# Transposing x by DMA instead of on TensorE, in a kernel that mixes a spectral filter and a dense layer

## The chip, the cores and the metric

The kernel runs on one core of a Trainium2 chip. Its engines are TensorE (PE; its weight loads are listed apart as PEld), VectorE (DVE), ScalarE (ACT), GpSimd (POOL) and SyncE (SP). SP, ACT and POOL also issue DMA transfers; each has a queue of its own, and all transfers run on the same 16 DMA engines. On-chip memory is SBUF; PE writes to PSUM, of which a bank holds 128 partitions x 512 numbers of 32 bits.

The metric is the time of one execution in microseconds (us). An execution under the profiler gives a span (first to last event) and the records quoted below.

## The reference

Input x has 2048 rows of 512 values (bf16). The output mixes two branches with a gate per row:

```python
g = sigmoid((x * gate_w).sum(-1, keepdims=True))
X = rfft2(x);  a = irfft2(X * (w_r + 1j*w_i))          # 2048 x 257 spectrum
h = x @ w1 + b1                                        # 512 -> 1792
b = (h * tanh(softplus(h))) @ w2                       # 1792 -> 512 (the activation is Mish)
out = g * a + (1 - g) * b
```

## The kernel before

x's 2048 rows are cut into 16 tiles of 128 rows (tile t holds the rows p*16 + t, p being the partition). The work falls into these steps; the names are those of the code.

- **Loads.** SP's queue brings x by rows into `xo` (`ld_x`, five transfers), w1 (`ld_w1`, four), the constants of the transforms (`ld_fd`, `ld_m1`, `ld_sm`, `ld_gd`) and the gate's weights. POOL's queue brings the filter W (`ld_W`, four transfers to 64 partitions each, 64 rows of 8224 bytes) and w2 (`ld_w2`, two). These wait for the last transfer of w1.
- **Transposes** (`tr`, L522). For each tile four 128x128 transposes on PE, by a matmul against a permutation matrix, into PSUM; DVE or ACT evicts them (`evx`) into `xT`, which has the 512 columns of x on partitions, as four blocks of 128.
- **First transform, over the columns.** For each pair of tiles DVE forms sums and differences of the four blocks (`ty`, `tz`, `t0`, `t2`), for each tile PE multiplies by cosines and sines (`a1`, L551 to L554) into bank 0, and an eviction (`e1`) writes `In1`.
- **s1** (L572): after every four tiles, a transform over 64 of the rows' index positions, evicted (`e2`) to `Ybuf` and written to a scratch tensor in DRAM (`r1w`, two transfers of 256 KB for each s1, eight in all, in pieces of 512 bytes).
- **s2** (L689): when all eight `r1w` have landed, the scratch is read back in another order (`r1r`, four transfers of 512 KB; the first s2 needs two of them), transformed over the remaining 32 positions, multiplied by W (`wm`, `wz` on DVE and POOL), transformed back (`s2i`, L732), and written to a second scratch (`r2w`). There are four rounds. A small piece, `s2x`, follows the first s2 and needs all of `r1r`.
- **s1i, a1i** (L764, L776): the second scratch is read back (`r2r`) and transformed back; ACT scales by the gate (`geo`) and DVE or POOL combine the halves (`ga`).
- **Dense branch.** `mm1` (L810): 56 outputs, each of four matmuls of 512 columns, to banks 6 and 7 in turn; `mish` on ACT writes `act`, with the bias b1 that a small PE transpose (`tr_small`, L529) turned into a column. `mm2` (L851, and L833 for the last tile, in halves): 14 matmuls for each tile.
- **Gate.** 16 dot products on DVE (`gdot`, from `xo`), a reorder by two tiny DMAs (`gdj`), a sigmoid (`gcol`) and `omg` = 1 - gate.
- **End.** For the first NBF = 12 tiles `mm2` is evicted scaled by `omg` (`bev`, into `xo`), and later summed with `ga` (`sum`); for the others one instruction does both (`fin`). The results are stored (`out`) by SP and, for the last tile, ACT.

The order of the instructions on each engine is fixed when the kernel is built, by a planner. Each step is a task with an estimated duration, priority and dependences that come from the tiles it reads and writes. `_Graph.schedule` repeatedly takes, among the tasks that can start within 0.1 us of the earliest, the one with the highest priority. Where a step may run on two engines, it goes to the one that would be done first. Transfers of a queue keep the order in which they were written; the planner models SP's and ACT's as one pipe and POOL's as a second, separate one, with a bandwidth given by each transfer (`bw`). Warm-up matmuls (L509) on a tile of zeros fill PE until the first `mm1`. At run time an engine works through its list in order and waits at semaphores; an instruction that waits holds all behind it on its engine.

Of the kernel before, what the change touches and what calls it, by code (L numbers as in the profile page):

```python
# [13 lines left out]
NT = 16  # L14
# [303 lines left out]
NBF = 12  # L318
# [4 lines left out]
def _build(nc, A_x, A_w_r, A_w_i, B_x, B_w1, B_b1, B_w2, gate_w, out):  # L323
# [11 lines left out]
    with es:  # L335
# [4 lines left out]
        xT = sb("xT", [128, 4, NT, 128], BF)  # L340
# [22 lines left out]
        pid = sb("pid", [128, 142], BF)  # L363
        perm, id14 = pid[:, 0:128], pid[0:14, 128:142]
# [35 lines left out]
        xv = A_x[0].rearrange("(p t) d -> p t d", t=16)  # L400
        ov = out[0].rearrange("(a b t) d -> b a t d", b=2, t=16)
# [15 lines left out]
        def dma(name, dst, src, reads=(), writes=(), nbytes=0, deps=(), is_out=False, prio=None, queue="sp", bw=300e3):  # L417
            dur = 1.0 if queue == "pool" else 0.5

            def fn(e, _dst=dst, _src=src):  # L420
                return e.dma_start(_dst, _src)

            t = G.add(name, queue, dur, fn, reads=reads, writes=writes, lat=2.0 + nbytes / bw, deps=deps, prio=prio)
            t.xfer = nbytes / bw
            t.isdma = True
            if is_out:
                t.sem = out_sem
                n_out_dma[0] += 1
                t.semval = 16 * n_out_dma[0]
            else:  # L430
                t.sem = new_sem("d_" + name)
                t.semval = 16
            return t

        def mm(n):
            return n / 2400.0 + 0.0025
# [13 lines left out]
        def evict(name, n, dst, src, reads, writes, prio=None):  # L450
# [6 lines left out]
        G.add("ones", "pool", 0.2, lambda e: e.memset(pid[:, :], 1.0), writes=["ones"])  # L457
        G.add("perm", "pool", 0.3, lambda e: e.affine_select(out=perm[:, :], in_=perm[:, :], pattern=[[-1, 2], [-2, 64]],
                                                             compare_op=ALU.is_equal, fill=0.0, base=0, channel_multiplier=1),
              reads=["ones"], writes=["perm"])  # L460
# [4 lines left out]
        def ld_x(t0, t1):  # L465
            dma(f"ld_x{t0}", xo[:, t0:t1, :], xv[:, t0:t1, :], writes=[("x", t) for t in range(t0, t1)], nbytes=128 * 1024 * (t1 - t0),
                bw=260e3 if t0 < 4 else 380e3)
# [12 lines left out]
        ld_x(0, 1)  # L480
        ld_x(1, 4)
# [4 lines left out]
        ld_x(4, 8)  # L486
        ld_m1(0)
        ld_w1(2)
        ld_x(8, 12)
        t_w1 = ld_w1(3)  # L490
        ld_x(12, 16)
# [8 lines left out]
        WALL = [("W", i, h) for i in range(2) for h in range(2)]  # L500
        for h in range(2):
            dma(f"ld_w2_{h}", w2_sb[:, 7 * h:7 * (h + 1), :], w2v[:, 7 * h:7 * (h + 1), :],
                writes=[("w2", h)], nbytes=128 * 7 * 1024, queue="pool", deps=[t_w1])
# [11 lines left out]
        t_r1w = []  # L515
        for t in range(NT):
            tbk = 1 + t if 1 <= t < 4 else 1

            def f_tr(e, t=t, tbk=tbk):
                ins = None  # L520
                for dt_ in range(4):
                    ins = e.transpose(psb[:, tbk, 128 * dt_:128 * (dt_ + 1)], xo[:, t, 128 * dt_:128 * (dt_ + 1)], perm[:, :])  # L522
                return ins

            t_tr = pe(f"tr{t}", 4 * mm(128), f_tr, reads=[("x", t), "perm"], writes=[("bank", tbk)], prio=SP0 + 1.0)
            evict(f"evx{t}", 512, xT[:, :, t, :], psb[:, tbk, 0:512].rearrange("p (r j) -> p r j", r=4),
                  [("bank", tbk)], [("xT", t)], prio=SP0 + 1.0)
            if t == 3:
                pe("tr_small", 0.1, lambda e: e.transpose(psb[:, 0, 0:14], braw[0:14, :], id14[:, :]),  # L529
                   reads=["braw", "id14"], writes=[("bank", 0)], deps=[t_tr], prio=SP0 + 1.0)  # L530
                G.add("ev_small", "dve", 0.2, lambda e: e.tensor_copy(out=b1f[:, :], in_=psb[:, 0, 0:14]), reads=[("bank", 0)], writes=["b1f"], prio=SP0 + 1.0)

            if t % 2 == 1:
# [6 lines left out]
                lo, hi = xT[:, 0:2, t0:t0 + 2, :], xT[:, 2:4, t0:t0 + 2, :]  # L540
                yy = yb[:, yi, :, :].rearrange("p r (t j) -> p r t j", t=2)
                xr = [("xT", t0), ("xT", t)]
# [5 lines left out]
        for t in range(NT):  # L548
            def f_a1(e, t=t):
                pr = ps[:, 0, :].rearrange("p (r x) -> p r x", r=4)  # L550
                e.matmul(pr[:, 0, :], Tb[:, 0, t, :], FDs[:, 0:128], start=True, stop=True)  # L551
                e.matmul(pr[:, 2, :], Tb[:, 1, t, :], FDs[:, 128:256], start=True, stop=True)
                for i in range(2):
# [5 lines left out]
               writes=[("bank", 0)], prio=SP0)  # L559
            evict(f"e1_{t}", 512, In1[:, t, :].rearrange("p (c r q) -> p c r q", c=2, r=4),  # L560
                  ps[:, 0, :].rearrange("p (r c q) -> p c r q", r=4, c=2),
                  [("bank", 0)], [("In1", t)], prio=SP0 + 0.2)
# [237 lines left out]
        for c in range(NCH):  # L800
            hb = c % 3
            G.cur_prio = PR['mm1c0'] if c == 0 else PR['mm1c'] - c
            for ft in range(NFT):
# [3 lines left out]
                def f_mm1(e, c=c, ft=ft, bank=bank):  # L807
                    ins = None
                    for dt_ in range(4):
                        ins = e.matmul(ps[:, bank, :], w1_sb[:, dt_, 128 * ft:128 * (ft + 1)],  # L810
                                       xT[:, dt_, 4 * c:4 * c + 4, :], start=(dt_ == 0), stop=(dt_ == 3))
                    return ins

                t_mm1 = pe(f"mm1_{c}_{ft}", 4 * mm(512), f_mm1,
                   reads=[("xT", 4 * c + i) for i in range(4)] + [("w1", ft)], writes=[("bank", bank)])
                if c == 0 and ft == 0:
                    G.filled = t_mm1
                G.add(f"mish_{c}_{ft}", "act", act_dur(512, True),
# [162 lines left out]
```

## Time and profile before

| | us |
|---|---|
| median of 3 runs (lowest, highest) | 142.38 (142.08, 142.75) |
| the profiled execution | 142.56 |
| its span | 140.8 |
| PE busy | 136.2 (97%) |
| DVE / ACT / POOL busy | 86.3 / 81.4 / 31.9 |
| bytes moved by DMA | 21.38 MB, 152 GB/s over the span |
| granted PE clock | 1.0 throughout |

The page lists the busy time of each engine and then the span in 40 slices of 3.52 us; a digit is the busy share in tenths. PE's times overlap, because matmuls are pipelined: one of 512 columns is listed with 380 ns, while in the chain four of them take 0.86 us. The chain that ended last follows the work back from the end, always to what released it. In the DMA view q1 is the hardware queue of SP, q0 the software queue of POOL, and a row of digits gives the busy share of the 16 engines in 40 equal parts of the stretch asked for. A DMA issue line gives the number of transfers, KB each, and the median time from issue to landing. A timeline line gives the start, the duration, the engine (SPq for SP's queue), the source line and what is written from what.

### The profile page before, as it was taken

The page shows a single profiled execution, that of the slowest core. Times are in us where ns is not written, and L with a number is a line of the kernel's source. Part 1 is how long each engine was busy: PE and PEld are TensorE (multiplying, and loading weights), DVE is VectorE, ACT ScalarE, POOL GpSimd, SP SyncE. Part 2 cuts the span into 40 slices and gives each one's busy share as a digit, 9 for nine tenths or more (in the row PEclk, how much of TensorE's full clock was granted, in tenths as well). Part 3 has the DMA queues.
Part 4 walks back from the last instruction along what each step waited for, and adds up shares of the span by engine and source line. Part 5 has one row for each costly group of instructions (what it writes and reads, how often), then busy time and mean ns, then how long its engine had stood idle before and what let it go on. Part 6 is the DMA issues. An engine that isn't in the chain of part 4 may idle for free.

```text
span 140.8 us, 2515 instructions
## 1 busy us (share of the span) xinstructions
PE 136.2 (97%) x946; PEld 74.2 (53%) x946; DVE 86.3 (61%) x192; ACT 81.4 (58%) x128; POOL 31.9 (23%) x62
## 2 busy tenths in 40 slices
PE   6999999999999999999999999999999999999991
PEld 4756656455544435435445444544444666766670
DVE  0276757748999303983983893592200499999831
ACT  4448797969874487488058437532411685776300
POOL 4000670003000001560440440340000144256400
PEclk9999999999999999999999999999999999999999
DMA  3999999999705485700300300300359615333422
GB/s 87 334 382 387 393 245 214 239 333 366 222 8 154 151 254 202 289 0 10 143 0 0 149 0 5 149 2 0 143 150 277 179 27 119 80 79 92 98 52 58
DMA packets 16556, 21.38 MB, mean 152 GB/s; under 512 B 1248, under 2 KB 12384, under 8 KB 16160
## 3 DMA queue, kind: packets, MB, share of 16 engines
q1 hardware_dynamic: 15552, 17.22, 39.3%
q0 software_dynamic: 832, 3.94, 10.4%
q8 instruction: 7, 0.11, 0.3%
q10 hardware_dynamic: 160, 0.07, 0.2%
q14 instruction: 5, 0.04, 0.1%
HBM read 14.92 MB, written 6.29 MB: 151 GB/s over the span
## 4 chain that ended last, share of the span: by engine, by line
PE 92%; ACT 4%; DVE 0%; issue 0%
PE ps L810 33%; PE ps L851 32%; PE ps L776 5%; PE ps L509 3%; PE ps L689 3%; PE ps L572 3%; PE ps L732 3%; PE ps L764 3%; PE ps L522 2%; ACT Ybuf L452 2%; PE ps L833 2%; PE ps L554 2%; ACT act L819 1%; PE ps L551 1%; ACT Abuf L452 1%; ACT xT L452 1%
## 5 line engine op out<-in xcount | busy, mean ns | idle before, releaser
L810 PE MATMUL ps<-xT,w_sb 128*128 128x512 bf16 x224 | 54.2, 380 | 0.4 <-ACT act L819 0.3
L819 ACT ACTIVATE act<-ps,b1f 128x512 bf16<-128x512 f32 x56 | 38.1, 690 | 21.8 <-PE ps L810 16.4
L851 PE MATMUL ps<-w_sb,act 128*128 128x512 bf16 x210 | 48.3, 379 | 0.0
L810 PEld LDWEIGHTS ps<-xT,w_sb 128*128 128x128 bf16 x224 | 20.0, 98 | 24.1 <-ACT act L819 5.7
L851 PEld LDWEIGHTS ps<-w_sb,act 128*128 128x128 bf16 x210 | 20.1, 98 | 22.4 <-issue 0.4
L699 DVE TENSOR_TENSOR misc<-ps,WT 128x512 f32<-128x512 f32 x32 | 19.9, 685 | 12.6 <-PE ps L689 12.6
L705 POOL TENSOR_TENSOR misc<-misc 128x255 bf16<-128x255 f32 x16 | 11.4, 731 | 41.0 <-DVE misc L699 41.0
L784 POOL TENSOR_TENSOR Tg<-misc 128x256 bf16<-128x256 f32 x12 | 10.3, 873 | 27.9 <-ACT misc L781 27.9
L790 ACT ACTIVATE xo<-ps,omg 128x512 bf16<-128x512 f32 x11 | 7.6, 687 | 15.2 <-PE ps L851 15.0
L451 DVE CAST Ybuf<-ps 128x512 bf16<-128x512 f32 (+1 forms) x10 | 8.8, 900 | 9.3 <-PE ps L732 8.2
L781 ACT ACTIVATE misc<-ps,gcol 128x512 f32<-128x512 f32 x16 | 10.3, 685 | 5.0 <-PE ps L776 4.0
L451 DVE CAST misc<-ps 128x512 bf16<-128x512 f32 x8 | 5.5, 683 | 11.4 <-PE ps L764 11.4
L784 DVE TENSOR_TENSOR Tg<-misc 128x256 bf16<-128x256 f32 x20 | 12.0, 629 | 0.7 <-ACT misc L781 0.7
L594 DVE SCALAR_TENSOR_TENSOR junk<-xo,gwb 128x512 bf16<-128x512 bf16 x16 | 11.0, 689 | 0.7
L452 ACT ACTIVATE Ybuf<-ps 128x512 bf16<-128x512 f32 (+1 forms) x14 | 9.4, 718 | 2.6 <-PE ps L572 1.6
L451 DVE COPY xT<-ps 128x512 bf16<-128x512 bf16 x10 | 4.2, 424 | 9.1 <-PE ps L522 9.0
L776 PE MATMUL ps<-GDs,misc 128*128 128x256 bf16 x64 | 9.3, 273 | 0.0
L452 ACT ACTIVATE Abuf<-ps 128x512 bf16<-128x512 f32 x12 | 7.2, 602 | 0.0
L776 PEld LDWEIGHTS ps<-GDs,misc 128*128 128x128 bf16 x64 | 6.0, 98 | 2.3
L522 PEld LDWEIGHTS ps<-pid,xo 128*128 128x128 bf16 x64 | 5.2, 110 | 3.0 <-issue 0.4
L522 PE MATMUL ps<-pid,xo 128*128 128x128 bf16 x64 | 6.7, 242 | 0.0
L705 DVE TENSOR_TENSOR misc<-misc 128x255 bf16<-128x255 f32 x16 | 6.4, 441 | 0.0
(81 smaller groups left out, 115.7 us busy)
## 6 DMA issues: line engine op xcount, KB each, us to landing
scr<-Ybuf SPq DMA_DIRECT2D x8, 256.0 KB, 9.3
Abuf<-scr SPq DMA_DIRECT2D x4, 512.0 KB, 4.5
scr<-Ybuf SPq DMA_DIRECT2D x4, 512.0 KB, 3.0
Abuf<-scr SPq DMA_DIRECT2D x8, 256.0 KB, 5.3
w_sb<-in_B_w_dram POOLq DMA_DIRECT2D x2, 896.0 KB, 17.5
out_dram<-xo SPq DMA_DIRECT2D x14, 128.0 KB, 2.3
w_sb<-in_B_w_dram SPq DMA_DIRECT2D x3, 512.0 KB, 7.9
xo<-in_A_x_dram SPq DMA_DIRECT2D x3, 512.0 KB, 8.7
```

The source lines that it names most:

```text
L451: G.add_multi(name, [("dve", dve_dur(n), lambda e: e.tensor_copy(out=dst, in_=src)), ("act", act_dur(n), lambda e: e.activation(dst, src, ...
L452: ("act", act_dur(n), lambda e: e.activation(dst, src, AF.Copy))],
L522: ins = e.transpose(psb[:, tbk, 128 * dt_:128 * (dt_ + 1)], xo[:, t, 128 * dt_:128 * (dt_ + 1)], perm[:, :])
L594: lambda e, t=t: e.scalar_tensor_tensor(out=junk[:, :], in0=xo[:, t, :], scalar=1.0, in1=gwb[:, :], op0=ALU.mult, op1=ALU.mult, accum_out= ...
L699: lambda e, Pb=Pb, Wu=Wu, bk=bk, pb=pb: e.tensor_tensor(out=Pb[:, pb, :].rearrange("p (c r q) -> p c r q", c=2, r=4), in0=ps[:, bk, :].rea ...
L705: fz = (lambda e, c=c, Pb=Pb, op=op, pb=pb, i=i, zb=zb: e.tensor_tensor(out=Zb[:, zb, i, c, 1:256], in0=Pb[:, pb, 1:256], in1=Pb[:, pb, 25 ...
L776: ins = e.matmul(ps[:, yk, 256 * (j // 2):256 * (j // 2) + 256], TT[:, ts_, j, :], GDs[:, j, :], start=(j % 2 == 0), stop=(j % 2 == 1))
L781: lambda e, t=t, gb=gb, yk=yk: e.activation(gEO[:, gb, :], ps[:, yk, :], AF.Copy, scale=gcol[:, t:t + 1]),
L784: fg = (lambda e, i=i, op=op, t=t, gb=gb: e.tensor_tensor(out=ga[:, t, 256 * i:256 * i + 256], in0=gEO[:, gb, 0:256], in1=gEO[:, gb, 256:5 ...
L810: ins = e.matmul(ps[:, bank, :], w1_sb[:, dt_, 128 * ft:128 * (ft + 1)], xT[:, dt_, 4 * c:4 * c + 4, :], start=(dt_ == 0), stop=(dt_ == 3))
L819: lambda e, ft=ft, bank=bank, hb=hb: e.activation(act[:, hb, ft, :], ps[:, bank, :], AF.Mish, bias=b1f[:, ft:ft + 1]),
L851: ins = e.matmul(ps[:, bank, :], act[:, hb, ft, 128 * tl:128 * (tl + 1)], w2_sb[:, ft, :], start=(ft == 0), stop=(ft == NFT - 1))
```

## The change

The 64 PE transposes of x, their permutation matrix and their 16 evictions are removed. Eight DMA transfers issued on ACT's queue, ahead of everything else there, read 64 rows x 2048 values (four tiles) of x each and write them transposed into `xT`, whose two middle dimensions change places so that a tile's four blocks lie together. The column sums on DVE and `mm1` read `xT` in the new layout.

`xo` is no longer loaded first. x is loaded by rows in four transfers of 512 KB on POOL's queue, after W and before w2, for the gate's dot products alone (and since `xo` holds results later). SP's queue has no transfer of x left, so w1 and the constants move up, and the third part of w1 now goes ahead of the first part of the constant M1.

`a1` writes banks 0 and 1 in turn. The bias transpose uses bank 5 and comes after the first `mm1`. NBF is 10. The planner is told 500 GB/s for x's and w2's transfers on POOL's queue and 250 GB/s for the transposing ones. The planner's new order follows from all of this: on PE 24 warm-ups, then `mm1` twice, four `a1`, and so on; all of s1 is placed earlier among the `mm1` than before, the first s2 comes after 27 `mm1` groups (of four matmuls) and no `mm2`, where before 33 groups of `mm1` and three of the half tiles of `mm2` (seven matmuls each) stood ahead of it. The last `mm2` tiles stand together at the end. On SP, `gdj` comes behind the first `r2w` instead of between the `r1r`.

```diff
@@ -315,7 +315,7 @@
-NBF = 12
+NBF = 10
 NWARM = 40
@@ -337,7 +337,7 @@
         xo = sb("xo", [128, NT, 512], BF)
-        xT = sb("xT", [128, 4, NT, 128], BF)
+        xT = sb("xT", [128, NT, 4, 128], BF)
         Tg = sb("Tg", [128, 8192], BF)
@@ -360,8 +360,7 @@
         omg = sb("omg", [128, NT], F32)
-        pid = sb("pid", [128, 142], BF)
-        perm, id14 = pid[:, 0:128], pid[0:14, 128:142]
+        id14 = sb("id14", [14, 14], BF)
         wrv = sb("wrv", [128, 2, 2, 16], BF)
@@ -398,6 +397,7 @@
         xv = A_x[0].rearrange("(p t) d -> p t d", t=16)
+        xtv = A_x[0].rearrange("(a b t) d -> b a (t d)", b=2, t=16)
         ov = out[0].rearrange("(a b t) d -> b a t d", b=2, t=16)
@@ -414,11 +414,11 @@
-        def dma(name, dst, src, reads=(), writes=(), nbytes=0, deps=(), is_out=False, prio=None, queue="sp", bw=300e3):
+        def dma(name, dst, src, reads=(), writes=(), nbytes=0, deps=(), is_out=False, prio=None, queue="sp", bw=300e3, transpose=False):
             dur = 1.0 if queue == "pool" else 0.5
             def fn(e, _dst=dst, _src=src):
-                return e.dma_start(_dst, _src)
+                return e.dma_start_transpose(_dst, _src) if transpose else e.dma_start(_dst, _src)
@@ -454,17 +454,16 @@
         G.cur_prio = 99.0
-        G.add("ones", "pool", 0.2, lambda e: e.memset(pid[:, :], 1.0), writes=["ones"])
-        G.add("perm", "pool", 0.3, lambda e: e.affine_select(out=perm[:, :], in_=perm[:, :], pattern=[[-1, 2], [-2, 64]],
-                                                             compare_op=ALU.is_equal, fill=0.0, base=0, channel_multiplier=1),
-              reads=["ones"], writes=["perm"])
+        G.add("ones", "pool", 0.2, lambda e: e.memset(id14[:, :], 1.0), writes=["ones"])
         G.add("id14", "pool", 0.2, lambda e: e.affine_select(out=id14[:, :], in_=id14[:, :], pattern=[[1, 14]],
-        def ld_x(t0, t1):
-            dma(f"ld_x{t0}", xo[:, t0:t1, :], xv[:, t0:t1, :], writes=[("x", t) for t in range(t0, t1)], nbytes=128 * 1024 * (t1 - t0),
-                bw=260e3 if t0 < 4 else 380e3)
+        def ld_xt(g):
+            for bx in range(2):
+                dma(f"ld_xt{g}{bx}", xT[:, 4 * g:4 * g + 4, :, 64 * bx:64 * bx + 64].rearrange("p t r j -> p (t r) j"),
+                    xtv[bx, :, 2048 * g:2048 * g + 2048], writes=[("xT", t, bx) for t in range(4 * g, 4 * g + 4)], nbytes=128 * 2048,
+                    queue="act", bw=250e3, transpose=True)
@@ -477,18 +476,17 @@
-        ld_x(0, 1)
-        ld_x(1, 4)
+        ld_xt(0)
         dma("ld_b1", braw[:, :], B_b1.rearrange("(ft p) -> ft p", p=128), writes=["braw"], nbytes=3584, queue="pool")
         ld_w1(1)
-        ld_x(4, 8)
+        ld_xt(1)
+        ld_w1(2)
+        ld_xt(2)
         ld_m1(0)
-        ld_w1(2)
-        ld_x(8, 12)
+        ld_xt(3)
         t_w1 = ld_w1(3)
-        ld_x(12, 16)
         ld_m1(1)
@@ -498,9 +496,13 @@
         WALL = [("W", i, h) for i in range(2) for h in range(2)]
+        for t0 in range(0, NT, 4):
+            dma(f"ld_x{t0}", xo[:, t0:t0 + 4, :], xv[:, t0:t0 + 4, :], writes=[("x", t) for t in range(t0, t0 + 4)], nbytes=128 * 4096,
+                queue="pool", deps=[t_w1], bw=500e3)
         for h in range(2):
             dma(f"ld_w2_{h}", w2_sb[:, 7 * h:7 * (h + 1), :], w2v[:, 7 * h:7 * (h + 1), :],
-                writes=[("w2", h)], nbytes=128 * 7 * 1024, queue="pool", deps=[t_w1])
+                writes=[("w2", h)], nbytes=128 * 7 * 1024, queue="pool", deps=[t_w1], bw=500e3)
@@ -513,23 +515,10 @@
         t_r1w = []
+        t_small = pe("tr_small", 0.1, lambda e: e.transpose(psb[:, 5, 0:14], braw[0:14, :], id14[:, :]),
+                     reads=["braw", "id14"], writes=[("bank", 5)], prio=SP0 + 2.0)
+        G.add("ev_small", "dve", 0.2, lambda e: e.tensor_copy(out=b1f[:, :], in_=psb[:, 5, 0:14]), reads=[("bank", 5)], writes=["b1f"], prio=SP0 + 2.0)
         for t in range(NT):
-            tbk = 1 + t if 1 <= t < 4 else 1
-            def f_tr(e, t=t, tbk=tbk):
-                ins = None
-                for dt_ in range(4):
-                    ins = e.transpose(psb[:, tbk, 128 * dt_:128 * (dt_ + 1)], xo[:, t, 128 * dt_:128 * (dt_ + 1)], perm[:, :])
-                return ins
-            t_tr = pe(f"tr{t}", 4 * mm(128), f_tr, reads=[("x", t), "perm"], writes=[("bank", tbk)], prio=SP0 + 1.0)
-            evict(f"evx{t}", 512, xT[:, :, t, :], psb[:, tbk, 0:512].rearrange("p (r j) -> p r j", r=4),
-                  [("bank", tbk)], [("xT", t)], prio=SP0 + 1.0)
-            if t == 3:
-                pe("tr_small", 0.1, lambda e: e.transpose(psb[:, 0, 0:14], braw[0:14, :], id14[:, :]),
-                   reads=["braw", "id14"], writes=[("bank", 0)], deps=[t_tr], prio=SP0 + 1.0)
-                G.add("ev_small", "dve", 0.2, lambda e: e.tensor_copy(out=b1f[:, :], in_=psb[:, 0, 0:14]), reads=[("bank", 0)], writes=["b1f"], prio=SP0 + 1.0)
             if t % 2 == 1:
@@ -537,9 +526,9 @@
-                lo, hi = xT[:, 0:2, t0:t0 + 2, :], xT[:, 2:4, t0:t0 + 2, :]
+                lo, hi = [xT[:, t0:t0 + 2, i:i + 2, :].rearrange("p t r j -> p r t j") for i in (0, 2)]
                 yy = yb[:, yi, :, :].rearrange("p r (t j) -> p r t j", t=2)
-                xr = [("xT", t0), ("xT", t)]
+                xr = [("xT", t0 + i, bx) for i in range(2) for bx in range(2)]
                 tt(f"ty{t}", yy, lo, hi, ALU.add, 512, xr, [("y", yi)])
@@ -547,7 +536,7 @@
             def f_a1(e, t=t):
-                pr = ps[:, 0, :].rearrange("p (r x) -> p r x", r=4)
+                pr = ps[:, t % 2, :].rearrange("p (r x) -> p r x", r=4)
                 e.matmul(pr[:, 0, :], Tb[:, 0, t, :], FDs[:, 0:128], start=True, stop=True)
@@ -556,10 +545,10 @@
             pe(f"a1_{t}", 2 * mm(128) + 2 * mm(256), f_a1, reads=[("T0", t), ("T2", t), ("Tz", t), "FD"],
-               writes=[("bank", 0)], prio=SP0)
+               writes=[("bank", t % 2)], prio=SP0)
             evict(f"e1_{t}", 512, In1[:, t, :].rearrange("p (c r q) -> p c r q", c=2, r=4),
-                  ps[:, 0, :].rearrange("p (r c q) -> p c r q", r=4, c=2),
-                  [("bank", 0)], [("In1", t)], prio=SP0 + 0.2)
+                  ps[:, t % 2, :].rearrange("p (r c q) -> p c r q", r=4, c=2),
+                  [("bank", t % 2)], [("In1", t)], prio=SP0 + 0.2)
@@ -808,13 +797,14 @@
                         ins = e.matmul(ps[:, bank, :], w1_sb[:, dt_, 128 * ft:128 * (ft + 1)],
-                                       xT[:, dt_, 4 * c:4 * c + 4, :], start=(dt_ == 0), stop=(dt_ == 3))
+                                       xT[:, 4 * c:4 * c + 4, dt_, :], start=(dt_ == 0), stop=(dt_ == 3))
                     return ins
                 t_mm1 = pe(f"mm1_{c}_{ft}", 4 * mm(512), f_mm1,
-                   reads=[("xT", 4 * c + i) for i in range(4)] + [("w1", ft)], writes=[("bank", bank)])
+                   reads=[("xT", 4 * c + i, bx) for i in range(4) for bx in range(2)] + [("w1", ft)], writes=[("bank", bank)])
                 if c == 0 and ft == 0:
                     G.filled = t_mm1
+                    t_small.deps.append(t_mm1)
                 G.add(f"mish_{c}_{ft}", "act", act_dur(512, True),
```

## The prediction

> **What bounds the kernel now.** I read the page first, then the chain of work that ended last in order of time, then the waits of the queues, then the DMA view cut into stretches.
>
> ```profile
> span 140.8 us, 2515 instructions
> PE 136.2 (97%) x946; PEld 74.2 (53%) x946; DVE 86.3 (61%) x192; ACT 81.4 (58%) x128; POOL 31.9 (23%) x62
> PE   6999999999999999999999999999999999999991
> DMA  3999999999705485700300300300359615333422
> ```
>
> TensorE is busy in every slice from the second on, so the end is set by the work on PE, in its fixed order, plus whatever makes PE wait. But the DMA row shows a second resource that is full from 3.5 to about 37 us. Today PE does not feel it. The chain shows why:
>
> ```profile
> 7.26 1.90 PE ps L810 x8
> 10.36 0.22 PE ps L522 x4
> 53.12 0.86 PE ps L810 x4
> 53.98 0.99 PE ps L689 x16
> 137.70 0.02 issue
> ```
>
> The first matmul of x with w1 (L810) starts at 7.26, and the first group of the second transform (L689, called s2 here) at 53.98, straight behind other work. s2 reads what went through DRAM: the first transform's result is written (r1w, eight transfers of 256 KB) and, when all eight have landed, read back (r1r). The DMA view from 17 to 32 us and from 32 to 46 us, and SP's reads:
>
> ```profile
> DMA  9999989999999699798995995997989999999999
> q0 software_dynamic: 630, 3.32, 86.4%
> q1 hardware_dynamic: 777, 0.65, 17.4%
> scr<-Ybuf SPq DMA_DIRECT2D x4, 256.0 KB, 14.9
> ...
> DMA  9999999999999995222100000000000099999300
> Abuf<-scr SPq DMA_DIRECT2D x1, 512.0 KB, 3.8
> ...
> 45.55 0.33 SPq L421 DMA_DIRECT2D Abuf<-scr  x1
> 48.48 1.53 SPq L421 DMA_DIRECT2D Abuf<-scr  x3
> ```
>
> From 17 to 32 us POOL's queue (W and w2) had 630 packets and SP's (r1w) 777: about one for one. But POOL's are large and r1w's are 512 B, so POOL held 86.4% of the engines and an r1w took 14.9 us to land. The second DMA row has slices of 0.35 us: fifteen nines, so the jam ended at 32 + 15 x 0.35 = 37.25 us. Until then everything issued had to pass. Since PE reached the last first-transform group only at 40.4, and s2 at 53.98, the jam cost nothing.
>
> **The change, part by part.** Sums are against the profiled execution, 142.56 us: span 140.82 and 1.76 around it; the median of the runs, 142.38, lies 0.18 below.
>
> *Transposes on PE go.* 64 matmuls of L522, sixteen groups; the twelve after 7.26 stand in the chain at 0.22 each: -2.66 us. Their evictions (ten of 0.42 on DVE, six of 0.60 on ACT) lie beside PE and only shorten waits. Between 7.26 and 53.98 (46.72 us) PE's work is 153 matmuls of 512 columns at 0.2155 (33.0), 16 of a1 at 0.335 (5.4), those 2.66, four s1 at 0.98 (3.9) and 0.04: 45.0. So 1.75 us of it is waits for evictions. The second bank for a1 and the lighter DVE and ACT can take between none and all of these.
>
> *Order.* The planner, no longer held by transposes, brings the spectral part forward: before s2 there were 153 matmuls of 512 columns, in the changed order 108. These 45 x 0.2155 = 9.70 us go behind s2. PE can thus be at s2 at 53.98 - 9.70 - 2.66 = 41.6 (39.9 without the 1.75), and from s2's start to PE's end it takes 83.72 + 9.70 = 93.4 us; then the tail, 140.82 - 137.70 = 3.1. The span is therefore s2's start + 96.5, and it equals the old one when s2 starts at 44.3. Everything hangs on whether r1r has landed by then.
>
> *x by transposing transfers, and again by rows.* Bytes of x go from 2.10 to 4.19 MB. The reload runs on POOL's queue between W and w2, ahead of the last r1w in practice, because POOL's large packets win the one-for-one turns. Its price is 2.10 MB at the 336 to 359 GB/s of the w2 stretch (28 to 36 us) or at the 383 to 394 of the first loads: 6.0 or 5.4; I take 5.7. The transposing transfers have no row. As plain loads they cost the 5.4 that their bytes cost now: +0. At the slowest full stretch (218 GB/s, 21.1 to 24.6 us) 9.6: +4.2. I take the 512 B packets' rate, 278 to 295 GB/s in the second DMA view, 7.2: +1.8, because a transfer that turns rows into columns moves short pieces. A gain is excluded: 394 is the best rate of any full stretch. The Trainium skill's pages differ here: "DMA: Bandwidth & Descriptors", Latency and other measured facts, has 261 GB/s for a transpose with a strided middle dimension (an estimate by it: 8.0 us, +2.6), "Advanced Engine Details and Errata", X-Bar Transpose, has 350 to 400 (about +0.2).
>
> *r1w and r1r.* Two of the eight r1w went after the jam; now all eight are in it, since PE ends the last s1 at about 7.26 + 12.1 + 5.4 + 3.9 + 1.75 = 30.4. Two times 0.26 MB at 290 GB/s: +1.8. So the last r1w lands at 37.25 + 5.7 + 1.8 + 1.8 = 46.6. s2 needs two r1r: the first alone took 3.8 from its issue, the second's 0.52 MB follows at 390 GB/s, 1.35; with 0.1 to issue, s2 starts at 51.8. PE waits 10 us there. The other two r1r land 2.7 later, when PE, after s2 (0.99) and eight matmuls (1.7), asks for them: 0.
>
> *PE cold after the wait.* The chain has eleven warm-up matmuls in 2.53 us at the start (0.23 each, 256 columns) where four of 256 columns take 0.44 in L776 (0.11); half speed lasts from 1.11 to about 6.5, a loss of 2.7 us. After 10 us of rest the loss is between 0 and 2.7; I take 2.0, nearer to the only start from rest that the trace has. The Trainium skill, "TensorE: Matmul & The Clock Gate", Part 1, says an idle window of about 3.4 us halves the clock and a busy one restores it: an estimate of 1.7 to 3.4 us by that; the trace shows the restoring, not the fall.
>
> *Issue on ACT.* Eight transfers at SP's 0.43 to 0.51 each put ACT's table load (1.28) off by 4 us, to 4.8; it is ready at 6.3, and its first eviction was due at 8.3. If each issue were held like SP's longest load issue (1.95), ACT would come 9.6 us late, and with it mish, the a1 evictions and PE. That is covered by the 10 us that PE waits at s2; without that wait it would cost up to 9.6. The same wait covers a late first matmul (xt0 and w1 now share the engines).
>
> *The rest, nothing.* x's pieces in the moving operand: L554 reads two runs of 128 columns at 0.11 per 256, as L776 reads one run. The bias transpose moves behind the first matmul, its eviction (0.17) ahead of the first mish. POOL issues four more DMAs (0.5 to 1.0 each) before copies that wait for W until 31.9 anyway. On SP the gate's two small transfers go from among the r1r to behind the first r2w; on DVE the dot products now wait for the reload, which lands ahead of w2, so before the wait at s2 ends. NBF 10: two tiles swap an eviction and a sum for one fused 0.75 us, beside 3.0 us of PE per tile. The tail is unchanged.
>
> *Sum.* 51.8 + 96.5 = 148.3; with 2.0 cold, 150.3; with 1.76 around it 152.1; at the median's level 151.9 us.
>
> The Trainium skill has a rule that speaks against this change: "DMA: Bandwidth & Descriptors", Rules for kernel authors, says that spreading transfers over SP, ACT and GpSimd brings no bandwidth, as all use the same 16 engines. The row above (86.4% and 17.4% in one stretch, the sum full) agrees; if each queue had its own room, the reload and the transposes would be free and the time 139.7, the next case.
>
> **The rivals.**
>
> *Faster.* The transfers fit: the reload is late enough, or r1w early enough, that r1r lands before PE comes at 41.6. Then the span is 41.6 + 96.5 = 138.1, without the old waits 136.4: 139.7 or 138.0 us. For it: r1w of the first groups is issued some us earlier. Against it: r1r would have to land before the reload's bytes could even have passed a full DMA. It decides at s2 before 44.3.
>
> *Near the old time.* r1w passes before w2 (1.84 MB, 5.2 us at 350 GB/s): s2 at 46.6, with transposes at plain cost 44.8, span 141.3 to 145.1 with or without the cold start: 142.9 to 146.7 us. Against it: the one-for-one turns.
>
> *Much slower.* If the transposing transfers' packets are small, POOL's 8 KB and 4 KB ones starve them as they starve r1w. Then the last part of x comes when POOL's queue drains, about 35 + 5.7 = 41. Behind it come DVE's steps (2 x 1.35), four a1 with evictions (3.0), s1 (1.0), eviction and r1w (4.1), r1r (5.2): s2 at 57, span 153.5, cold starts 2 to 4, so about 158 us.
>
> *It doesn't do what it says:* excluded, since the 64 matmuls are gone from PE's order.
>
> **How the numbers follow.** The forecast (jam to about 45 to 49 us; 148 to 155) has 0.56, faster 0.14, near the old 0.10 (0.04 within 0.5%, about what a measurement can tell from no change), much slower 0.20. The range runs from 141.0, above most of the faster case, to 160.0, above most of the slow one; the forecast's own, from the ends of the transposes' and the cold start's price, is 148.1 to 155.0.
>
> **What would show it.** L522 gone; s2 near 52 with the longest wait of PE before it, ended by r1r; DMA full to about 45 us; q0 above 80% from 17 to 40 us; matmuls of 512 columns at twice 0.2155 for some us after the wait; from s2 to PE's end 93.4 (95.4 with the cold start). It is wrong if s2 starts before 45, or if PE waits more in the first 30 us for x or ACT than at s2.

## The result: 25% slower, and the time is lost before s2

| | before | after |
|---|---|---|
| median (lowest, highest), us | 142.25 (142.08, 142.75), 4 runs | 177.88 (176.59, 179.31), 4 runs |
| ratio, 95% interval | 1 | 1.247 (1.239, 1.255) |
| the profiled execution, us | 142.56 | 177.53 |
| its span | 140.8 | 175.8 |
| start of s2 | 53.98 | 78.95 |
| s2's start to the end of PE | 83.7 | 93.7 |

The ratios here and in experiment 7 leave out the slowest run of the changed kernel (179.31) and of that experiment's kernel (150.32), each over 1.5% above the fastest of its kernel.

Lines of the changed kernel have other numbers: `mm1` is L799 (was L810), `mm2` L841 (L851), `a1` begins at L540 (L551), `s1` is L561 (L572), `s2` L678 (L689), ACT's table load L509 (L507). The head of the page, and its rows of 40 slices of 4.4 us:

```profile
span 175.8 us, 2380 instructions
PE 136.3 (78%) x876; PEld 71.0 (40%) x885; DVE 85.6 (49%) x186; ACT 74.9 (43%) x116; POOL 33.6 (19%) x65
PE   7409000000799999999999999999999999999992
PEclk9956755555579999999999999999999999999999
DMA  5999999999304443595220030020379134110222
```

PE's busy time is as before (136.2), but spread over 35 us more. There are two holes: a short one in the third slice (8.8 to 13.2 us), and a long one from the fifth to the tenth (17.6 to 44); after it there is no zero until the end. The DMA row is full until the end of the long hole, about 44 us. The forecast had a jam to about 45 us, but that its end fits is luck: the r1w counted into it come only from 53.9 us on, and the transposing transfers took longer. The granted clock falls to 0.5 in the holes. Pieces of the chain that ended last, in order of time up to s2 (start, duration, what; most of those on PE between 44 and 71 us are left out):

```profile
0.80 1.35 ACTq L421
2.17 1.81 ACTq L421
4.00 4.06 ACTq L421
8.09 6.64 ACTq L421
14.77 5.18 ACTq L421
19.97 1.74 ACTq L421
21.74 15.77 ACTq L421
37.54 5.35 ACTq L421
42.92 1.28 ACT L509
46.49 3.41 PE ps L799 x8
71.72 7.23 PE ps L799 x32
78.95 0.99 PE ps L678 x16
```

The first eight pieces are not transfers but ACT itself, issuing them: 42.1 us, one of them 15.77. Only then does ACT load its table (1.28) and begin to evict. s2 follows directly on `mm1` matmuls: the wait for r1r that was forecast is not there. The waits say who stood for ACT (engine, line, releaser: us in total, times, longest):

```profile
ACT L509 <- issue: 42.9, 1, 42.9
PE ps L540 <- ACT Abuf L452: 27.4, 1, 27.4
DVE yb L526 <- DMA xT<-in_A_x_dram: 12.5, 1, 12.5
```

The last line is the short hole: the first tiles of x landed only at 13.4. PE did two groups of `mm1` and two `a1`, and then waited 27.4 us with the third `a1`: it writes bank 0, and the planner had given the eviction of that bank's first result to ACT. Why the issues took so long shows in the DMA view of 31 to 41 us, inside the issue of 15.77 us and the next (q10 is ACT's queue, q0 POOL's; packets, MB, share of the engines):

```profile
DMA packets 1786, 3.56 MB, mean 356 GB/s; under 512 B 989, under 2 KB 989, under 8 KB 1770
q0 software_dynamic: 893, 3.33, 91.8%
q10 hardware_dynamic: 893, 0.23, 11.1%
```

893 against 893: the two queues took turns one for one, with pieces of 256 bytes on one side and nearly all of 4 KB (a few of 8) on the other. In 10 us ACT's queue moved 0.23 MB, 23 GB/s. Two stretches, the long hole and all from s2's start to PE's end (stretch, length, busy us of PE, PEld, DVE, ACT and POOL with their instructions, granted clock, DMA share, GB/s):

```profile
17.50:45.00 27.50, 0.16 (x2) 0.00 (x0) 0.69 (x1) 2.07 (x4) 8.13 (x20) 0.54 1.08 292
79.00:172.70 93.70, 93.04 (x613) 49.02 (x620) 58.86 (x114) 46.76 (x70) 24.28 (x38) 1.00 0.27 80
```

From s2 to PE's end it is 93.7 us with PE full; the whole of the miss lies ahead of s2.

### The profile page after: what moved, and what is told of

It is laid out like the page before. It is cut to its first block, busy times and chain, and to the rows that moved or that the text cites. A ratio compares the mean times of both kernels' runs of the same rounds, so it can differ in the third digit from the quotient of the medians.

```text
span 175.8 us, 2380 instructions
## 1 busy us (share of the span) xinstructions
PE 136.3 (78%) x876; PEld 71.0 (40%) x885; DVE 85.6 (49%) x186; ACT 74.9 (43%) x116; POOL 33.6 (19%) x65
## 3 DMA queue, kind: packets, MB, share of 16 engines
q0 software_dynamic: 1408, 6.04, 11.6%
## 4 chain that ended last, share of the span: by engine, by line
PE 72%; ACTq 24%; ACT 1%; issue 1%; DVE 0%
PE ps L799 29%; PE ps L841 25%; ACTq L421 24%; PE ps L765 4%; PE ps L678 2%; PE ps L561 2%; PE ps L721 2%; PE ps L543 2%; PE ps L753 2%; PE ps L823 2%; PE ps L540 1%; ACT L509 1%; PE ps L541 1%; ACT Abuf L452 0%; DVE xo L830 0%
## 5 line engine op out<-in xcount | busy, mean ns | idle before, releaser
L799 PE MATMUL ps<-xT,w_sb 128*128 128x512 bf16 x224 | 55.7, 396 | 7.2 <-issue 7.2
L841 PE MATMUL ps<-w_sb,act 128*128 128x512 bf16 x201 | 46.2, 379 | 0.5 <-issue 0.2
L809 ACT ACTIVATE act<-ps,b1f 128x512 bf16<-128x512 f32 x56 | 38.1, 688 | 14.7 <-PE ps L799 13.4
L799 PEld LDWEIGHTS ps<-xT,w_sb 128*128 128x128 bf16 x224 | 20.2, 101 | 36.2 <-issue 11.5
L841 PEld LDWEIGHTS ps<-w_sb,act 128*128 128x128 bf16 x210 | 20.1, 98 | 22.7 <-DVE xo L851 0.3
L540 PE MATMUL ps<-FDs,Tg 128*128 128x128 bf16 x16 | 3.9, 241 | 27.4 <-ACT Abuf L452 27.4
L694 POOL TENSOR_TENSOR misc<-misc 128x255 bf16<-128x255 f32 x16 | 11.4, 728 | 64.9 <-DVE misc L688 64.9
L451 DVE CAST Abuf<-ps 128x512 bf16<-128x512 f32 x7 | 4.8, 688 | 31.7 <-PE ps L543 31.7
L451 DVE CAST Ybuf<-ps 128x512 bf16<-128x512 f32 (+1 forms) x11 | 9.5, 882 | 9.1 <-PE ps L721 5.1
L540 PEld LDWEIGHTS ps<-FDs,Tg 128*128 128x128 bf16 x16 | 1.7, 108 | 29.3 <-issue 28.3
L779 ACT ACTIVATE xo<-ps,omg 128x512 bf16<-128x512 f32 x9 | 6.2, 688 | 17.1 <-PE ps L841 17.1
L451 DVE CAST misc<-ps 128x512 bf16<-128x512 f32 x8 | 5.5, 683 | 11.4 <-PE ps L753 11.3
L526 DVE TENSOR_TENSOR yb<-xT 128x512 bf16<-128x512 bf16 x8 | 3.3, 417 | 12.5 <-DMA xT<-in_A_x_dram 12.5
L851 DVE SCALAR_TENSOR_TENSOR xo<-ps,omg,Tg 128x512 bf16<-128x512 f32 x5 | 3.7, 749 | 8.6 <-PE ps L841 7.9
## 6 DMA issues: line engine op xcount, KB each, us to landing
w_sb<-in_B_w_dram SPq DMA_DIRECT2D x3, 512.0 KB, 10.9
```

Source lines behind the costliest of these rows:

```text
L451: G.add_multi(name, [("dve", dve_dur(n), lambda e: e.tensor_copy(out=dst, in_=src)), ("act", act_dur(n), lambda e: e.activation(dst, src, ...
L694: fz = (lambda e, c=c, Pb=Pb, op=op, pb=pb, i=i, zb=zb: e.tensor_tensor(out=Zb[:, zb, i, c, 1:256], in0=Pb[:, pb, 1:256], in1=Pb[:, pb, 25 ...
L809: lambda e, ft=ft, bank=bank, hb=hb: e.activation(act[:, hb, ft, :], ps[:, bank, :], AF.Mish, bias=b1f[:, ft:ft + 1]),
L841: ins = e.matmul(ps[:, bank, :], act[:, hb, ft, 128 * tl:128 * (tl + 1)], w2_sb[:, ft, :], start=(ft == 0), stop=(ft == NFT - 1))
```

## Experiments

The theory after the result: ACT is held while it issues a transposing transfer, because the small pieces issued before still wait for their turns; beside larger packets that takes many times longer; and since PE's order puts everything behind evictions by ACT, PE stands. Its rivals: the transposing transfers are as slow when nothing is beside them; or ACT's holding doesn't matter, as x itself comes just as late. The first six kernels are the changed one with the order of a few transfers altered after the planner; in all of them these names are used:

```diff
         order = G.schedule()
+        by = {t.name: t for t in G.tasks}
+        xts = [by[f"ld_xt{g}{bx}"] for g in range(4) for bx in range(2)]
```

The first six are one profiled execution each; the last two were timed repeatedly. The kernel before took 142.05 us beside the first four and 142.45 (median of 8) beside the last four.

**1. The transposes alone on the DMA engines.**

```diff
+        by["ld_w1_0"].deps += xts
```

> SP's first load, and with it all behind it on SP and what POOL loads after w1, waits until all eight transposing transfers have landed; the order of every engine is that of the changed kernel. Three theories. Starved: a transposing transfer is cut into pieces of 256 bytes which take turns, one for one, with the larger packets of the other queues, and ACT is held while they are. Slow by itself: each issue takes its 1.3 to 15.8 us whatever else runs. Late data: only the landing of x matters, not that ACT is held. Starved expects the eight issues to take 9 to 12 us in all instead of 42.1 (8192 pieces of 18 ns on 16 engines are 9.2) and the last to land at 11 to 13. Slow by itself expects about 42 again. Late data says nothing on it. The time itself is not the point; as the loads all begin some 12 us late it should be near 155.

Measured: 162.35 us. All issues of the line (shortest/median/longest in ns):

```profile
L421 ACTq DMA_TRANSPOSE xT<-in_A_x_dram x8: 1344/1351/1448, 0.8 to 10.5; - x8
```

and the DMA view from 2 to 13 us:

```profile
DMA packets 7979, 1.98 MB, mean 180 GB/s; under 512 B 7979, under 2 KB 7979, under 8 KB 7979
q10 hardware_dynamic: 7947, 1.98, 94.1%
```

Alone, each issue takes 1.35 us and ACT is done after 11.1 us in place of 42.1. So the transposes are not by themselves what holds ACT for 42 us. They are not cheap either: an issue takes three times that of a plain load on SP (0.43 to 0.51), and 94.1% of the engines' time goes for 180 GB/s, where plain loads moved 383 to 394 in the kernel before. With w1 held back PE waits 11.4 us for w1, W starts at 26.2, and s2 comes at 61.1 after a wait of 7.0 for r1r: the DMA path is the bound again. The time is 7 us above the 155 that was expected for it.

**2. POOL's large loads wait; SP's remain beside the transposes.**

```diff
+        by["ld_W00"].deps += xts
```

> The changed kernel, in which POOL's loads of W, x and w2 wait also for the last transposing transfer; SP's loads still run beside them. Starved expects that the issues on ACT end at about 23 to 25 instead of 42.9 (about a third has passed when SP's loads end at 18, the rest goes alone at some 280 GB/s), that ACT starts at 25 and the first s2 at about 59, held by the reading back of the first scratch, so a time near 158. Slow by itself expects 42.1 us of issue and 178 or more.

Measured: 162.70 us.

```profile
L421 ACTq DMA_TRANSPOSE xT<-in_A_x_dram x8: 1347/1768/6892, 0.8 to 24.4; - x8
```

The issues take 24.95 us together, the longest 6.9. By subtraction, of the 42.1 us some 11 are the transposes alone, 14 come with SP's loads beside them, and 17 with POOL's. PE's wait for ACT at `a1` falls from 27.4 to 9.2 us. W now starts at 28.9, and s2 at 64.0, behind a wait of 2.9 for r1r. The time is some 5 us above what was expected for it: as in experiment 1, W comes late, and with it the loads that follow it on POOL's queue.

**3. The transposes on SP's queue, spread among w1 and the constants.** ACT is free.

```diff
+        order["act"] = [t for t in order["act"] if t not in xts]
+        loads = [by[n] for n in ("ld_xt00 ld_xt01 ld_w1_0 ld_fd ld_w1_1 ld_xt10 ld_xt11 ld_w1_2 ld_xt20 ld_xt21 "
+                                  "ld_m1_0 ld_xt30 ld_xt31 ld_w1_3").split()]
+        order["sp"] = loads + [t for t in order["sp"] if t not in loads]
```

> The eight transposing transfers are issued on SP's queue instead, mixed with w1 and the constants in the order in which the program names them and all ahead of the last part of w1, so that POOL's loads begin behind them. PE, DVE, ACT and POOL keep their order. Starved expects the transfers to land by about 20 and ACT to be ready at 2.5; then the full DMA engines are the next bound, as forecast for the change: the first s2 at about 53, after a wait for the reading back of the scratch, a time near 152. Late data expects the same delay as on ACT's queue as far as x lands late, and a time well over 165; slow by itself expects SP to be held for some 40 us, w1 with it, and more than 175.

Measured: 159.30 us, 7 above what the theory expected, and below what the rivals expected (over 165 and over 175). SP issues the eight transposes in 14.7 us together. The longest wait of PE is now the forecast one:

```profile
PE ps L678 <- DMA Abuf<-scr: 11.6, 1, 11.6
```

s2 starts at 58.3. Three stretches of this kernel, the wait, the 5.8 us behind it and the rest up to PE's end, show the cold start in the granted clock, the third column from the right (columns as above):

```profile
46.80:58.20 11.40, 0.00 (x0) 0.00 (x0) 2.27 (x8) 0.64 (x1) 0.00 (x0) 0.63 0.73 226
58.20:64.00 5.80, 5.72 (x37) 2.90 (x38) 3.19 (x7) 1.05 (x2) 1.42 (x2) 0.56 0.64 243
64.00:154.40 90.40, 89.82 (x577) 47.24 (x584) 55.33 (x105) 44.98 (x68) 22.87 (x36) 1.00 0.25 73
```

58.2 to 154.4 is 96.2 us, 2.5 more than the 93.7 of the changed kernel, whose PE was warm at s2. The wait and the round trip are of the forecast's kind, but s2 is 6.5 us later than its 51.8. Where that comes from shows in POOL's queue (start, duration, what, and what it waited for), first of the kernel before:

```profile
15.32 1.12 POOL L421 DMA_DIRECT2D WT<-in_A_w_r_dram  x2 [12.46 <-DMA w_sb<-in_B_w_dram]
```

and then of this one:

```profile
23.69 1.12 POOL L421 DMA_DIRECT2D WT<-in_A_w_r_dram  x2 [21.24 <-DMA w_sb<-in_B_w_dram]
```

W may start when the last part of w1 is in, and that is 8.4 us later, because the transposes are ahead of w1 and take longer than plain loads. The forecast had 1.8 for it. Of the 6.5 that s2 is late, 5.2 are there when the last r1w has landed (51.8, forecast 46.6); the reading back then takes 6.4, forecast 5.25.

This kernel shows also that it needs no transposing transfer to hold an engine. Beside POOL's loads one issue of r1w, a plain write in pieces of 512 bytes, held SP for 11.4 us, and in the kernel before one (at 26.3 us, in the full stretch) for 4.46. The row of the kernel before, then of this one:

```profile
L421 SPq DMA_DIRECT2D scr<-Ybuf x12: 359/513/4457, 17.0 to 99.6; - x12
```

```profile
L421 SPq DMA_DIRECT2D scr<-Ybuf x12: 359/514/11386, 21.9 to 105.9; - x12
```

**4. The same, but the transposes after the first start behind all of w1.**

```diff
-        loads = [by[n] for n in ("ld_xt00 ld_xt01 ld_w1_0 ld_fd ld_w1_1 ld_xt10 ld_xt11 ld_w1_2 ld_xt20 ld_xt21 "
-                                  "ld_m1_0 ld_xt30 ld_xt31 ld_w1_3").split()]
+        loads = [by[n] for n in ("ld_xt00 ld_xt01 ld_w1_0 ld_fd ld_w1_1 ld_w1_2 ld_m1_0 ld_w1_3 "
+                                  "ld_xt10 ld_xt11 ld_xt20 ld_xt21 ld_xt30 ld_xt31").split()]
```

> As the run with the transfers on SP's queue, but six of the eight (all but those of the first four tiles) go behind the last part of w1, so that they meet POOL's loads; ACT is free. This keeps the starving and takes away the holding of ACT. Starved expects x's last part to land only when POOL's queue has drained, at 38 to 44, SP held until then, PE waiting for x instead of ACT, the first s2 at 55 to 60 and a time of 154 to 160: the holding of ACT is then worth the rest, some 18 to 24 us. Late data expects about 178, as the last part of x lands no earlier than in the changed kernel.

Measured: 166.04 us.

```profile
L421 SPq DMA_TRANSPOSE xT<-in_A_x_dram x8: 1297/2406/17050, 0.8 to 35.3; - x8
```

```profile
DVE yb L526 <- DMA xT<-in_A_x_dram: 26.3, 3, 14.8
PE ps L540 <- DVE Tg L526: 20.5, 2, 14.6
```

POOL's loads run beside the transposes again, and SP is held in its turn: its longest issue is 17.05 us. ACT is free, but x comes late, DVE waits 26.3 us for it and PE 20.5 for DVE. s2 is at 67.5, where 55 to 60 was expected: that left out the 28 matmuls of `mm1` that stand among the last `a1` and `s1` (6.0 us), the 52 between the last `s1` and s2 (11.2), and the cold PE. So both halves cost: the starved x puts s2 at 67.5 even with a free ACT, against 58.3 in experiment 3. The changed kernel's 11.9 us more than this one is not all ACT's holding, since the last of x also landed 2.9 us earlier here (42.85 against 45.73). If those 2.9 are taken off in full, some 9 us are left for the holding (an estimate from the two kernels); the rival that only x's landing matters had expected about 178 here.

**5. Experiment 3 without the reload.**

```diff
-                  lambda e, t=t: e.scalar_tensor_tensor(out=junk[:, :], in0=xo[:, t, :], scalar=1.0, in1=gwb[:, :],
+                  lambda e, t=t: e.scalar_tensor_tensor(out=junk[:, :], in0=xT[:, t].rearrange("p r j -> p (r j)"), scalar=1.0, in1=gwb[:, :],
...
+        reload = [by[f"ld_x{t0}"] for t0 in range(0, NT, 4)]
+        order["pool"] = [t for t in order["pool"] if t not in reload]
...
```

> The run with the transposing transfers on SP's queue, without the second load of x: the gate's dot products are taken of the transposed tile instead, so the gate is computed of other data (the same number and kind of instructions, in the same order). There the first s2 stood at 58.3 us after a wait of 11.6 for the reading back of the scratch. If full DMA engines set that wait, as the prediction's second step had it, the reload costs its 5.4 to 6.0 us there: s2 at 52.3 to 52.9, time 153 to 154. If the scratch's traffic is held by its turns against single large packets or by something else than bytes, s2 moves by less than 3 us.

Measured: 152.88 us, s2 at 52.5.

```profile
PE ps L678 <- DMA Abuf<-scr: 6.1, 1, 6.1
```

s2 comes 5.8 us earlier than in experiment 3, and the wait for r1r is 5.5 shorter: the second read of x is paid in full, as long as PE waits for r1r.

**6. Experiment 5 with w2 behind r1r.**

```diff
+        w2 = [by["ld_w2_0"], by["ld_w2_1"]]
+        w2[0].deps += t_r1r
+        pool = [t for t in order["pool"] if t not in w2]
+        k = pool.index(by["wcols"]) + 1
+        order["pool"] = pool[:k] + w2 + pool[k:]
```

> The run without the reload, and in it w2's two transfers (1.84 MB) wait on POOL's queue for the reading back of the scratch. If the bytes set the wait, it goes away: PE reaches the first s2 at about 46.7, when it reached it in the run with the reload, and finds the data there or within 2 us; PE does not get cold, s2 to PE's end takes 93.7 instead of 96.2, and the time is 146 to 148. That would still be slower than before, for PE starts its first matmul of x later (8.3 instead of 7.3, and at half speed) and waits for W. If not the bytes, the time stays above 150.

Measured: 148.02 us, s2 at 47.6.

```profile
PE ps L799 <- DMA w_sb<-in_B_w_dram: 2.1, 1, 2.1
PE ps L721 <- POOL misc L711: 1.8, 1, 1.8
PE ps L678 <- DMA Abuf<-scr: 1.7, 1, 1.7
```

The wait at s2 is 1.7 us and PE stays warm. What is left above the kernel before, 5.6 us, is spread, by the waits seen: a late first `mm1`, this wait and those for w1 and POOL (1.8 us behind s2, where POOL issues w2); no run takes it apart further. So even without the reload and with w2 out of the way the transposing loads don't reach the old time in this order.

**7. The kernel before, with two banks for a1.** No transposing transfer and no reload: only the other part of the change, the earlier first transform. The later tiles' PE transposes get two other banks, and the planner makes a new order.

```diff
-            tbk = 1 + t if 1 <= t < 4 else 1
+            tbk = 1 + t if 1 <= t < 4 else 2 + t % 2
-                pr = ps[:, 0, :].rearrange("p (r x) -> p r x", r=4)
+                pr = ps[:, t % 2, :].rearrange("p (r x) -> p r x", r=4)
```

(with the writes and the eviction of `a1` likewise)

> The kernel before with one part of the change alone: a1 in banks 0 and 1 in turn (the later tiles' transposes on PE go to banks 2 and 3 in turn, since bank 1 is taken). The order is planned anew. The prediction gave the waits for evictions between the first matmul of x and s2 as 1.75 us, of which the second bank can take none to all: 140.6 to 142.4. Against it: the new order brings the first transform forward by some 10 us, into the full DMA stretch; with all of the scratch's writes inside it, it ends at about 39, and the data for s2 would be there at 44 to 45, so PE may wait some 2 us: up to 144.

Measured: 148.79 us (147.91 to 150.32, 4 runs), ratio 1.043 (1.038, 1.047): slower, and above all of the 140.6 to 144 that was expected. The chain before s2:

```profile
33.66 3.62 PE ps L810 x16
37.60 4.41 DMA scr<-Ybuf
42.48 5.83 DMA Abuf<-scr
48.45 1.92 PE ps L689 x16
```

The planner moved s2 ahead of `mm1` and `mm2` work: as in the changed kernel, 27 groups of `mm1` and no `mm2` stand before it, and PE ran out of work at 43.7. But the round trip through DRAM had only begun with the last r1w's start at 37.6 and took 10.9 us. PE waited 4.8 us, and from 48.4 to its end took 95.7, a cold start again. s2 started 5.5 us earlier, but 12.0 us more lay behind it than the 83.7 of the kernel before, and the kernel lost 6. The old order, with its 33 groups of `mm1` before s2, hid this round trip: there PE asked for r1r's data only at 53.98.

**8. The kernel before, with two banks for the transposes only.**

```diff
-            tbk = 1 + t if 1 <= t < 4 else 1
+            tbk = 1 + t if 1 <= t < 4 else 4 + t % 2
```

> The kernel before, a1 in its one bank, with the later tiles' transposes on PE in banks 4 and 5 in turn instead of bank 1 alone. It takes the wait of a transpose for the eviction of the one before it. Of the 1.75 us of waits none to half: 141.4 to 142.4; s2 stays where it is, so no DMA stretch is met.

Measured: 141.69 us (141.21 to 141.77, 5 runs), ratio 0.994 (0.992, 0.996): 0.6% less, a small difference but clear of 1, and the fastest kernel here. s2's start is at 54.0 as before. The stretch from s2 to PE's end, first of the kernel before and then of this one:

```profile
53.98:137.70 83.72, 83.70 (x577) 44.95 (x577) 54.57 (x103) 42.36 (x65) 24.07 (x38) 1.00 0.30 89
```

```profile
54.00:136.90 82.90, 82.85 (x573) 44.63 (x573) 54.57 (x104) 41.71 (x64) 24.06 (x38) 1.00 0.30 90
```

Four matmuls of 512 columns (0.86 us) have moved from behind s2 to ahead of it, and s2 is no later for them; so PE had that much idle time ahead of s2 less. That a transpose no longer waits for the eviction of the one before fits this; the order is also a new one, and no run separates the two. The matmuls did not have to leave PE for it.

**What the runs add up to.** With s2 behind 27 groups of `mm1` each profiled time is s2's start plus 98.5 to 101.2 us (93.7 to PE's end, 3.1 of tail and 1.8 around the span, up to 2.5 for a cold PE, or in experiment 6 the wait of 1.8 for POOL):

| kernel | s2 starts | time, us | what ends before s2 |
|---|---|---|---|
| before | 54.0 | 142.3 | PE's own work |
| changed | 78.95 | 177.9 | ACT held by issues, then PE's work |
| 4: on SP, starved by POOL | 67.5 | 166.0 | x, then PE's work |
| 3: on SP, ahead of POOL | 58.3 | 159.3 | r1r |
| 5: and no reload | 52.5 | 152.9 | r1r |
| 6: and w2 behind r1r | 47.6 | 148.0 | r1r, little |
| 7: PE transposes, but a new order | 48.4 | 148.8 | r1r |

## Why the prediction was wrong

The direction was right and the time 26 us too low. 27.1 us lie between the forecast start of s2 (51.8) and the measured one (78.95), and the price of the transposing transfers made them, in two steps: their issue and their landing. The experiments put it in this order: ahead of POOL's loads and with ACT free s2 starts 6.5 us late (experiment 3), beside POOL's loads and with ACT free 15.7 (experiment 4), and issued by ACT 27.1.

- **Issue on ACT: the step that failed.** Its upper bound was 1.95 us for each transfer, SP's longest load issue, so 9.6 us of delay, covered by the wait at s2. Measured were 42.1 us in all, up to 15.77 for one. The row was that of a load in pieces of 4 KB. The forecast had itself found that small packets starve beside POOL's large ones, and did not ask what the engine that issues them does meanwhile. The trace of the kernel before had the row for it, the issues of r1w in pieces of 512 bytes, of which one held SP for 4.46 us (shown with experiment 3). Eight times that would have been 35.7 us, an estimate that puts ACT far beyond the cover of 10. The cover failed as well: the wait at s2 covers only what PE can do while it waits, and in its fixed order everything behind the third `a1` needed ACT.
- **Much slower** had the mechanism (one-for-one turns, x's last part at 41) and not the size. 158 us counted x's landing and the steps behind it. It left out that ACT is held until then, and the `mm1` matmuls that PE's order puts before s2 (17.2 us for the 28 and the 52 of experiment 4), which could not run during the wait.
- **x by transposing transfers: the other step that failed.** +1.8 us, with ends at 0 and +4.2, was too low at both, and it had no term for the turns against POOL's packets, which the forecast left to a rival. Alone, 2.1 MB took 11.1 us where plain loads take 5.4, so +5.7; experiment 3 shows W 8.4 us late. The Trainium skill's two figures for such transfers ("DMA: Bandwidth & Descriptors", Latency and other measured facts, 261 GB/s, and "Advanced Engine Details and Errata", X-Bar Transpose, 350 to 400) both lie above the 180 GB/s measured here with nothing beside them; the measurement decides. The forecast took the rate of the 512 B packets; the pieces are half as long (0.23 MB in 893). Beside POOL's loads the last of x landed at 42.85 us with ACT free and at 45.73 in the changed kernel.
- **And again by rows.** 5.7 forecast; 5.8 is the difference at s2 between experiments 3 and 5.
- **Order.** 93.4 from s2's start to PE's end forecast, 93.7 measured, and 3.1 for the tail. The 45 matmuls behind s2 were as counted.
- **r1w and r1r.** The forecast's wait at s2 is not in the changed kernel. It appears as soon as ACT is free: 11.6 us in experiment 3, for 10 forecast. That s2 then starts at 58.3 and not at 51.8 is for the most part the price of the transposes, by which the jam ends later.
- **PE cold after the wait.** 2.0 forecast, 2.5 measured in experiment 3. The trace now shows the fall too: 0.63 granted in 11.4 us of rest, 0.56 in the 5.8 after it, then 1.00. That agrees with what the Trainium skill says ("TensorE: Matmul & The Clock Gate", Part 1: an idle window halves the clock until a busy one restores it). For the cold start that the forecast took its price from, the clock row reads 1.0; there only the matmuls' doubled times show it.
- **Transposes on PE go.** The matmuls went, but the 1.75 us of waits for evictions became one wait of 27.4 for ACT. How much of the 1.75 the second bank would have freed can't be read from this kernel. Experiment 8 got 0.8 us in the old one, by other banks.
- **A late first matmul.** The first `mm1` came at 13.5 instead of 7.26; the forecast had put such a delay down to the cover at s2. PE had run warm-ups until 6.3 and then rested, so its first matmuls were also at half speed (3.2 us for eight, where 1.9 was the old price). In the changed kernel this lies within ACT's 42 us; in experiments 3, 5 and 6 the first `mm1` was late too, and in 6 that is part of the 5.6 that remain.
- **Faster** and **near the old time** needed r1r by 44.3 to 46.6. Experiment 7 shows that this fails without any transposing transfer: with s2 behind the same 27 groups of `mm1`, r1r's data came at 48.3, and PE waited 4.8 us for them.

The sign of being wrong that the prediction named, a longer wait of PE in the first 30 us for x or ACT than at s2, is what the profile shows: PE waits for ACT from 17.5 us on, and at s2 not at all.

## What to carry to other kernels

Price a transfer not only by its bytes but by how long the issuing engine is held by it, and look for that in the rows of transfers with pieces of the same size: a transfer in small pieces belongs on a queue whose engine has nothing due, and not beside large packets of another queue. A wait that covers a delay covers it only for work that the waiting engine's order lets run in the meantime; follow the order behind the first instruction that waits. Before work is brought forward, compare the new due time of what it reads with the whole round trip that brings it, from the last write's issue on.

## What the runs showed of the hardware

- The engine that issues a transposing transfer of 256 KB, in pieces of 256 bytes, is held 1.35 us when nothing else moves, up to 6.9 us beside SP's loads and up to 15.8 (ACT) or 17.05 us (SP) beside POOL's, in rows where most plain loads on SP take 0.43 to 0.51.
- It is not the transposing alone: plain writes of 256 KB in pieces of 512 bytes held SP for up to 4.46 us in the kernel before and 11.4 in experiment 3, both beside POOL's loads.
- The engine is not held until its transfer has landed: the one whose issue took 15.77 us landed 23.1 us after the issue began. That it waits for room in its queue fits all of these: counted from the DMA records of the changed kernel and of experiments 1 and 2, between 1024 and 1927 of ACT's pieces had still to move at the end of each of the 24 issues, one to two transfers of 1024. No run varies that.
- From 31 to 41 us of the changed kernel the turns between two queues were one for one in packets (893 to 893) although the sizes differed, so the smaller pieces got 0.23 MB of 3.56.
- Transposing transfers alone moved 180 GB/s with the engines 94% busy, about half of what plain loads moved.
